# A strided-attention and gated-FFN kernel: h of the last seven chunks by seven block products of 256 columns (Strassen's identity)

## The chip, the cores and the metric

One core of one Trainium2 chip. The metric is device time in microseconds of one execution of the whole kernel; lower is better. The engines named below are TensorE (PE, with its weight loads PEld), VectorE (DVE), ScalarE (ACT), GpSimd (POOL) and SyncE (SP), which issues most transfers.

## The reference

Attention over 8 batches of 8 heads, 576 rows, width 64, with a local mask for heads 0 to 3 and a strided mask for heads 4 to 7; its output, seen as 4608 rows of 512, goes through a feed-forward layer with 2048 hidden columns.

```
scores = scale * np.matmul(q, k.transpose(0, 1, 3, 2))
mask_local = (rel >= 0) & (rel < 32)
mask_strided = (rel >= 0) & (pos[None, :] % 32 == pos[:, None] % 32)
attn = softmax(np.where(masks, scores, -1e9));  x = (attn @ v) as (4608, 512)
h = x @ w_in                                   # 512 -> 2048
sp = np.maximum(h, 0.0) + np.log1p(np.exp(-np.abs(h)))
g = h * erf(sp)
return g @ w_out                               # 2048 -> 512
```

## The kernel before, in words

x is worked on in nine chunks of 512 rows: chunk b (0 to 7) is the first 512 rows of batch b, and chunk 8 collects the 64 rows that each batch has left over, which `stash` puts into the DRAM tensor `rests` and `reload` brings back. A chunk has 16 f-tiles of 128 hidden columns. Every fp32 operand is held as two float32r parts, a high one and the low rest (`xhi`/`xlo`, `pair[:, 0]`/`pair[:, 1]`, `ghi`/`glo`), and a product is made of three matmul terms: high by high, low weight by high, high weight by low.

`ftile` (one per chunk and f-tile) issues, in this order of dependence: 12 matmuls of 512 columns for h (four blocks of 128 of x's 512 columns, three terms, L914) into a PSUM bank; a DVE copy `hs` out of that bank (L922); softplus and erf on ACT (L925, L928), each with a table load per two f-tiles; the product a*hs on DVE (L931); the split of the result into `ghi` on ACT (L934) and `glo` on DVE (L937); and 12 matmuls of 512 columns for the output (four banks o0 to o3 of 128 rows, three terms, L980). After the 16th f-tile ACT evacuates the four banks and SP stores them.

Attention for batches 2 to 7 runs between the f-tiles: `burst` is one run of TensorE that multiplies the weights of one pair of heads with v and makes the scores of the next pair; `Pair.soft` is the softmax between, over DVE, ACT and POOL, with a transpose and an exchange `pt<-tt` of quarters through SP (L766). The first two batches are done ahead of the f-tiles by `heads`. `weight` turns the 64-bit weights into the two float32r parts, on DVE (three bit operations and a subtraction on 128x1024) and ACT.

The order on each engine is written by `Plan.order()`, a list scheduler that starts, of the operations that are ready, the one with the lowest key; the keys are tables of numbers (`FE`, `FT`, `KP`, ...). Each engine then runs its list strictly in that order. While the first f-tiles wait, the plan fills TensorE with dummy matmuls `warm` (L1143).

Of the kernel before, what the change touches and what calls it, by code (L numbers as in the profile page):

```python
# [60 lines left out]
KP = (
    (-19.871, -19.772, -18.081, 66.367, -18.136, 66.385, -21.044),
    (-20, -19.783, -18.109, -17.925, 66.357, -18.175, 65.821),
    (-20.011, -20.022, -18.1, -17.903, -17.836, -17.915, -18.021),
    (-19.805, -19.783, -18.131, 65.874, 66.629, 66.053, 66.246),
    (-17.104, -8.328, 50.311, 2195.03794, 66.246, 102.21, 68.625),
    (-19.761, -19.772, 66.052, -18.121, -18.137, 102.19, 102.261),
    (-17.222, -16.968, 68.835, 66.436, 68.835, 50.29, -17.926),
    (-19.75, -19.88, 66.257, 68.556, 68.856, 66.235, 65.932),
    (-16.968, 102.961, 74.711, 2202.59494, 2202.66194, 2240.33894, 2239.52794),  # L70
    (66.961, 2240.52794, 160.089, 2239.27294, 2251.46194, 31.017, 102.239),
    (31.228, 2312.70894, 184.489, 146.19, 2428.50594, 103.15, 102.328),
    (2312.71994, 103.339, 208.889, 2293.98794, 2306.33394, 103.217, 207.07),
    (103.439, 2330.76494, 8023.49621, 2257.52794, 2312.35094, 237.161, 176.808),
    (2459.68094, 103.439, 245.489, 255.672, 236.95, 2434.38194, 2348.29394),
    (2330.75394, 103.428, 245.478, 2355.10594, 102.854, 2349.06194, 333.672),
    (237.518, 237.507, 294.289, 2294.26294, 2397.84494, 2397.86194, 2415.89494),
    (237.496, 103.45, 7811.28821, 2416.10594, 2434.37094, 341.673, 2300.35194),
    (334.761, 335.139, 343.089, 2446.64494, 2452.53794, 2397.66194, 2458.56994),
    (2301.36294, 2459.58094, 361.389, 2458.71894, 2428.48394, 102.843, 2409.99594),  # L80
    (2459.65894, 2459.58094, 391.889, 2410.20694, 2489.36694, 2397.75094, 2458.54794),
    (2459.65894, 2459.65894, 8103.71921, 2513.71694, 2647.99494, 2513.76194, 2531.83094),
    (2459.65894, 2593.93694, 440.689, 2532.02094, 2532.10994, 432.372, 2550.19594),
    (432.539, 432.528, 465.089, 377.967, 2556.41194, 341.973, 2568.36194),
    (433.262, 432.561, 483.389, 2568.57294, 2574.76694, 529.8, 529.45),
    (432.939, 432.561, 513.889, 2593.14494, 2599.13394, 2550.31194, 529.45),
    (573.961, 2593.92594, 538.289, 2623.41994, 529.95, 2629.68394, 572.839),
    (2661.09094, 573.95, 562.689, 2641.76194, 529.889, 2647.98394, 603.373),
    (530.439, 573.839, 574.889, 2568.76294, 529.939, 2647.97294, 603.483),
    (470.441, 2661.05794, 8229.05321, 603.532, 2648.06194, 725.161, 529.006),  # L90
    (573.828, 627.561, 635.889, 2733.27794, 2733.36694, 627.939, 724.25),
    (627.55, 2599.05394, 660.289, 2757.79494, 529.928, 2598.84294, 626.85),
    (823.161, 2599.03194, 678.589, 670.65, 670.7, 627.739, 724.35),
)
# [1162 lines left out]
```

## Time and profile before

| | |
|---|---|
| time, median of 3 runs | 891.66 us (891.28 to 893.11) |
| span of the profiled execution | 890.8 us |
| TensorE busy in it | 872.9 us, 7436 matmuls |
| VectorE, ScalarE busy | 504.0 us, 590.8 us |
| bytes moved by DMA | 75.24 MB |

The span runs from the first to the last instruction of the profiled execution; the median of the runs lies 0.9 us above it. A busy TensorE in the profile overlaps successive matmuls, so the rate of a stream is read from the starts of its matmuls in the timeline, not from the mean duration of one.

### The profile page before, as it was taken

To read this page: it belongs to the slowest core of one execution; us is meant where nothing else is said; L and a number is where in the kernel's file an instruction comes from. 1 tells how busy PE (TensorE), PEld (TensorE's weight loads), DVE (VectorE), ACT (ScalarE), POOL (GpSimd) and SP (SyncE) were. 2 spreads that over 40 slices of the span, in tenths; PEclk is the share of its full clock that TensorE was granted. 3 is DMA by queue.
4 is the path that set the end of the run, shared out by engine and by line. 5 is a ranking of instruction groups with operands and counts; after the bars stand their busy time and mean duration, and the time that the engine had idled before them with its cause. 6 is when DMAs were issued, how large, how long until landed. Compare 5 with 4: busy or idle time off the path is not lost.

```text
span 890.8 us, 18132 instructions
## 1 busy us (share of the span) xinstructions
PE 872.9 (98%) x7436; PEld 716.2 (80%) x7436; DVE 504.0 (57%) x799; ACT 590.8 (66%) x878; POOL 120.6 (14%) x157
## 2 busy tenths in 40 slices
PE   6899999999999999999999999999999999999997
PEld 4677888888888888888888888888888888888886
DVE  5989994556565555655555555555556433343432
ACT  4887786676676667666666677666766565466653
POOL 2210000132221110102112111121112200000000
PEclk9999999999999999999999999999999999999999
DMA  9997010151332122212321222112311310001001
GB/s 346 368 363 261 1 48 7 59 119 58 89 88 71 59 72 96 73 57 72 104 73 56 74 88 79 45 30 72 100 68 32 105 47 1 1 1 47 1 1 47
DMA packets 37266, 75.24 MB, mean 84 GB/s; under 512 B 12960, under 2 KB 16288, under 8 KB 37184
## 3 DMA queue, kind: packets, MB, share of 16 engines
q1 hardware_dynamic: 34576, 69.24, 23.0%
q0 software_dynamic: 2448, 4.59, 2.7%
q8 instruction: 58, 0.95, 0.4%
q10 hardware_dynamic: 160, 0.26, 0.1%
q14 instruction: 24, 0.20, 0.1%
HBM read 56.12 MB, written 13.63 MB: 78 GB/s over the span
## 4 chain that ended last, share of the span: by engine, by line
PE 69%; issue 21%; DVE 3%; ACT 3%; DMA 3%; SPq 0%; POOL 0%; POOLq 0%; ACTq 0%; DVEq 0%
PE h L914 32%; PE o L980 30%; PE x L682 3%; PE s L662 2%; DMA qk<-qk_str 1%; PE s L536 1%; DVE pair L883 1%; ACT L928 1%; ACT L925 1%; PE s L409 1%; DMA out<-ob 1%; PE s L516 0%; DVE a L931 0%; DVE w L869 0%; DMA rests<-xhi 0%
## 5 line engine op out<-in xcount | busy, mean ns | idle before, releaser
L980 PE MATMUL o<-pair,ghi 128*128 128x512 f32 x1152 | 358.2, 392 | 0.3 <-DVE xlo L560 0.3
L914 PE MATMUL h<-xhi,pair 128*128 128x512 f32 x1152 | 287.6, 392 | 1.3 <-DVE a L931 0.8
L914 PEld LDWEIGHTS h<-xhi,pair 128*128 128x128 f32 x1152 | 216.1, 188 | 48.4 <-DVE a L931 1.8
L980 PEld LDWEIGHTS o<-pair,ghi 128*128 128x128 f32 x1152 | 214.1, 188 | 45.7 <-DVE xlo L560 0.5
L980 PE MATMUL o<-pair,glo 128*128 128x512 f32 x576 | 224.3, 389 | 0.0
L934 ACT CAST ghi<-a 128x512 fp32r<-128x512 f32 x144 | 89.2, 621 | 169.8 <-PE o L980 155.0
L922 DVE COPY hs<-h 128x512 f32<-128x512 f32 x128 | 88.0, 687 | 131.6 <-PE h L914 131.5
L914 PE MATMUL h<-xlo,pair 128*128 128x512 f32 x576 | 155.0, 391 | 0.0
L937 DVE TENSOR_TENSOR glo<-a,ghi 128x512 fp32r<-128x512 f32 x144 | 100.7, 700 | 77.8 <-ACT ghi L934 75.7
L931 DVE TENSOR_TENSOR a<-a,hs 128x512 f32<-128x512 f32 x128 | 88.7, 730 | 88.6 <-ACT a L928 88.6
L914 PEld LDWEIGHTS h<-xlo,pair 128*128 128x128 f32 x576 | 108.7, 189 | 22.7
L980 PEld LDWEIGHTS o<-pair,glo 128*128 128x128 f32 x576 | 108.1, 188 | 22.6
L925 ACT ACT_TABLE_LOAD x83 | 106.5, 1283 | 21.9 <-DVE hs L922 20.7
L925 ACT ACTIVATE a<-hs 128x512 f32<-128x512 f32 x128 | 80.8, 632 | 54.5 <-DVE hs L922 46.9
L739 POOL TENSOR_TENSOR sm<-sm,r 128x640 f32<-128x640 f32 (+1 forms) x24 | 35.4, 1475 | 468.3 <-DVE r L736 433.3
L928 ACT ACT_TABLE_LOAD x72 | 92.4, 1283 | 1.3
L928 ACT ACTIVATE a<-a 128x512 f32<-128x512 f32 x144 | 83.8, 625 | 0.8
L761 POOL COPY pt<-tt 32x320 f32<-32x320 f32 (+1 forms) x96 | 57.8, 602 | 46.1 <-DVE tt L745 42.6
L719 DVE TENSOR_TENSOR s<-s,con 128x640 f32<-128x640 f32 (+1 forms) x24 | 21.6, 899 | 37.4 <-PE s L662 37.4
L745 DVE STREAM_TRANSPOSE tt<-sm 128x320 f32<-128x320 f32 (+1 forms) x48 | 23.2, 522 | 19.4 <-POOL sm L739 19.4
L682 PEld LDWEIGHTS x<-pt,v 64*64 64x64 f32 x1392 | 24.4, 134 | 8.5 <-issue 8.5
L728 ACT ACT_TABLE_LOAD x24 | 30.8, 1283 | 0.4
(68 smaller groups left out, 503.1 us busy)
## 6 DMA issues: line engine op xcount, KB each, us to landing
v<-v_loc SPq DMA_DIRECT2D x16, 640.0 KB, 5.4
qk<-qk_loc SPq DMA_DIRECT2D x16, 592.0 KB, 5.2
words<-w_in SPq DMA_DIRECT2D x8, 1024.0 KB, 11.3
words<-w_out SPq DMA_DIRECT2D x8, 1024.0 KB, 7.8
out<-ob SPq DMA_DIRECT2D x32, 256.0 KB, 2.3
qk<-qk_res SPq DMA_DIRECT2D x12, 656.0 KB, 5.7
v<-v_str SPq DMA_DIRECT2D x16, 384.0 KB, 4.4
qk<-qk_str SPq DMA_DIRECT2D x4, 608.0 KB, 7.9
```

The source lines that it names most:

```text
L682: yield nc.tensor.matmul(self.x[m][d, n * a : n * (a + 1)], self.v[rows, (2 * a + h) * D : (2 * a + h) * D + D], p, start=True, stop=True,)
L728: yield nc.scalar.activation(sm[:, :, :cols], sm[:, :, :cols], AF.Exp, scale=1.0 / D**0.5)
L739: yield nc.gpsimd.tensor_tensor(out=wide(sm), in0=wide(sm), in1=spread(rc), op=ALU.mult)
L761: yield nc.gpsimd.tensor_copy(pt[quarter(m, f), f, :], plane(m, f, f))
L914: yield nc.tensor.matmul(ph[:, :CH], win[f // 2][:, w, 2 * P * cc + f0 : 2 * P * cc + f0 + P], x[cc][:, c0 : c0 + CH], start=(lo and i == ...
L922: yield nc.vector.tensor_copy(hs.tile, ph.tile)
L925: yield nc.scalar.activation(a.tile, hs.tile, AF.Softplus)
L928: yield nc.scalar.activation(a.tile, a.tile, AF.Erf)
L931: yield nc.vector.tensor_tensor(out=a.tile, in0=a.tile, in1=hs.tile, op=ALU.mult)
L934: yield nc.scalar.copy(ghi.tile, a.tile)
L937: yield nc.vector.tensor_tensor(out=glo.tile, in0=a.tile, in1=ghi.tile.bitcast(F32), op=ALU.subtract)
L980: yield nc.tensor.matmul(po.tile, g[:, ts], wout[f // 2][:, w, f % 2 * SW : f % 2 * SW + SW], start=(f == first_f and i == 0), stop=(f == ...
```

## The change

Chunks 0 and 1 are done as before. From chunk 2 on, two f-tiles are done together by `fpair`. With the 512 rows of x in two halves of 256, the 512 inputs in two halves of 256 (each two blocks of 128) and the 256 hidden columns in two f-tiles, the 2x2 block product is made with Strassen's identity in Winograd's form: seven block products, each of 6 matmuls of 256 columns (three terms by two blocks of 128 inputs). So h of two f-tiles takes 42 matmuls of 256 columns (L1016) where it took 24 of 512. The second matmul (now `second`, L1168) stays as it is.

What this needs around it: `prepare` (once per pair of f-tiles and half) makes the four weight sums S1 to S4 on DVE and ACT and stores them with the three unchanged blocks into the DRAM tensor `blocks`; `stream` loads the seven blocks of a pair, 256 KB each, for every pair of every chunk, into two alternating sets of buffers; `convert` makes the sums of x's blocks and their high and low parts, once per chunk and half of the inputs, from an fp32 copy `raw` that ACT takes out of PSUM (L841) in place of the split; and `fpair` makes h out of the products in the two PSUM banks X and Y: one ACT copy (L1046), five DVE additions (L1037) and a DVE copy (L1056) of 128x256 take the place of the two `hs` copies. The keys of the plan are new throughout, those of the first chunks too.

```diff
+    def prepare(i, k, pair, ready, before, key):
+        ...
+        def sums():
+            a11, a12, a21, a22 = "S2", "S4", "S3", "S1"
+            for out, a, b, op in (("S1", a21, a22, ALU.add), ("S3", a11, a21, ALU.subtract),
+                                  ("S2", "S1", a11, ALU.subtract), ("S4", a12, "S2", ALU.subtract)):
+                yield nc.vector.tensor_tensor(out=piece(out), in0=piece(a), in1=piece(b), op=op)
...
+        o = add("dve", 0.15 + 4 * P / 960.0, key, whole, [ready, *before], [made], [pair])
+        o = add("dve", 4 * (0.1 + P / 960.0), key + 0.1, sums, [o], [], [made])
+        o = add("act", 0.2 + 4 * P / 1200.0, key - 2095.0, s_hi, [o], [], [made])
+        o = add("dve", 0.15 + 4 * P / 960.0, key + 0.2, s_lo, [o], [], [made])
+        out = [add("sp", P * 8 * SW / 3.9e5, key - 2090.0, store_made, [o], [], [made])]
...
+    def convert(c, k, raw, ready_a, ready_b, key):
...
+        o1 = add("dve", d, key, minus("t1", "b12", "b11"), ready_a, [], [raw])
+        o3 = add("dve", d, key + 0.01, minus("b12", "b22", "b12"), [o1, *ready_b], [], [raw])
+        o2 = add("dve", d, key + 0.02, minus("t2", "b22", "t1"), [o1, *ready_b], [], [raw])
+        o4 = add("dve", d, key + 0.03, minus("t4", "b21", "t2"), [o2], [], [raw])
+        out = []
+        for i, n, t, o in ((0, 4, ta, o3), (1, 3, tb, o4)):
+            o = add("act", 0.2 + n * HALF / 1200.0, key + CV[1] + 0.1 * i, hi(i), [o], [t], [raw])
+            out.append(add("dve", 0.15 + n * HALF / 960.0, key + 0.1 + 0.1 * i, lo(i), [o], [], [raw, t]))
...
+    def stream(n, j, key):
...
+        def load(dst, u, m=1):
+            def run():
+                yield nc.sync.dma_start(dst(), blocks_d[j][:, u : u + m])
...
+    def fpair(c, j, ts, ready, w_ready, after_burst):
...
+        def products(todo):
+            def run():
+                for dst, half, x, t, first in todo:
+                    w = unit(units, x)
+                    i, y = place[t]
+                    terms = [(p, q, kk) for p, q in ((0, 0), (1, 0), (0, 1)) for kk in range(2)]
+                    for e, (p, q, kk) in enumerate(terms):
+                        yield nc.tensor.matmul(
+                            dst[:, half * HALF : half * HALF + HALF], w[:, kk, p], ts[kk][i][:, y, q],
+                            start=first and e == 0, stop=e == len(terms) - 1, skip_group_check=True,
+                        )
...
+        p16 = pe(0, [(X, 0, "A11", "B11", True), (X, 1, "S2", "T2", False)], [*ready, *mm1_first[-1:], *after_burst], [X], [])
+        p57 = pe(1, [(Y, 0, "S1", "T1", True), (Y, 1, "S3", "T3", False)], [p16], [Y], [])
...
+        p1 = add("act", 0.2 + HALF / 1200.0, v0 + SUM[0], first_sum, [p16], [u], [X])
+        u2 = add("dve", d, v0 + SUM[1], plus(lambda: u[:, :HALF], lambda: X[:, HALF:], lambda: u[:, HALF:]), [p1], [], [X, u])
+        t5 = add("dve", d, v0 + SUM[1], plus(lambda: u[:, HALF:], lambda: Y[:, :HALF], lambda: u[:, :HALF]), [p57, u2], [], [Y, u])
+        c22 = add("dve", d, v0 + SUM[2], plus(lambda: u[:, HALF:], lambda: Y[:, HALF:], lambda: u[:, HALF:]), [t5], [], [Y, u])
+        p2 = pe(2, [(X, 0, "A12", "B21", False)], [p57, u2], [], [X])
+        p34 = pe(3, [(Y, 0, "S4", "B22", False), (Y, 1, "A22", "T4", False)], [p2, c22], [], [Y])
...
+        c11 = add("dve", d, v0 + SUM[3], keep, [p2, u2], [hs[0]], [X])
+        c12 = add("dve", d, v0 + SUM[3], plus(lambda: hs[0][:, HALF:], lambda: Y[:, :HALF], lambda: u[:, :HALF]), [p34, c11], [], [Y, u, hs[0]])
+        c21 = add("dve", d, v0 + SUM[4], plus(lambda: u[:, :HALF], lambda: Y[:, HALF:], lambda: u[:, :HALF]), [p34, c12], [], [Y, u])
```

The softplus, erf, product and split of the two f-tiles follow `c12` and `c21` as before. A burst of attention now stands after every second pair, and the products of the next pair stand behind it.

The order on TensorE in chunk 5 before: the last of h of one f-tile (h, L914), then the output matmuls (o, L980) of an earlier f-tile, then h of the next.

```order
L914 MATMUL h_5916<-xlo_83,pair_1123 128x512
L914 MATMUL h_5916<-xlo_84,pair_1123 128x512
L980 MATMUL o_80_5690<-pair_1345,ghi_5885 128x512 x2
L980 MATMUL o_80_5690<-pair_1345,glo_5887 128x512
L980 MATMUL o_80_5720<-pair_1345,ghi_5885 128x512 x2
L980 MATMUL o_80_5720<-pair_1345,glo_5887 128x512
L914 MATMUL h_5946<-xhi_77,pair_1455 128x512
```

The order on TensorE in chunk 5 now, at the third step of one pair: the end of the second step (hy is bank Y, L1016), the third step (hx is bank X), two groups of output matmuls (L1168), and the first two matmuls of the fourth step. ta_0 and ta_1 are the converted halves of x, u the streamed weight blocks.

```order
L1016 MATMUL hy_7438<-ta_0_5856,u_7182 128x256
L1016 MATMUL hy_7438<-ta_1_6557,u_7182 128x256
L1016 MATMUL hx_7418<-ta_0_5856,u_29_7306 128x256
L1016 MATMUL hx_7418<-ta_1_6557,u_29_7306 128x256
...
L1168 MATMUL o_80_6933<-pair_1417,ghi_7327 128x512 x2
L1168 MATMUL o_80_6933<-pair_1417,glo_7331 128x512
L1168 MATMUL o_80_6950<-pair_1417,ghi_7327 128x512 x2
L1168 MATMUL o_80_6950<-pair_1417,glo_7331 128x512
L1016 MATMUL hy_7438<-ta_0_5856,u_7182 128x256
L1016 MATMUL hy_7438<-ta_1_6557,u_7182 128x256
```

The h work of two f-tiles, which stood in two groups of 12 with output matmuls between, now stands in steps of 12, 12, 6 and 12 shorter ones, and the third step follows the second with nothing between; it has to wait for a sum on DVE that reads the first step's bank.

The order on DVE around the second and third prepared weight before: the products a (L931) and low parts glo (L937) of f-tiles 2 and 3 of the first chunk, among the weight work (L862 to L883).

```order
L875 SCALAR_TENSOR_TENSOR w_2_806<-words_531,w_2_806 128x1024
L931 TENSOR_TENSOR a_956<-a_956,h_808 128x512
L560 TENSOR_TENSOR xlo_81<-s_0_840,xhi_77 128x256
L560 TENSOR_TENSOR xlo_81<-s_0_840,xhi_77 128x320
L931 TENSOR_TENSOR a_947<-a_947,h_887 128x512
L883 TENSOR_TENSOR pair_1051<-w_9_942,pair_1051 128x1024
L937 TENSOR_TENSOR glo_1080<-a_947,ghi_1076 128x512
```

The same place on DVE now (L1254 is the product, L1260 the low part, L1120 to L1141 the weight work).

```order
L1141 TENSOR_TENSOR pair_940<-w_9_899,pair_940 128x1024
L1120 TENSOR_SCALAR w_3_1016<-words_915 128x1024
L1127 SCALAR_TENSOR_TENSOR w_3_1016<-words_915,w_3_1016 128x1024
L1133 SCALAR_TENSOR_TENSOR w_3_1016<-words_915,w_3_1016 128x1024
L1141 TENSOR_TENSOR pair_997<-w_2_925,pair_997 128x1024
L1120 TENSOR_SCALAR w_6_1075<-words_938 128x1024
L1141 TENSOR_TENSOR pair_1072<-w_3_1016,pair_1072 128x1024
L1127 SCALAR_TENSOR_TENSOR w_6_1075<-words_938,w_6_1075 128x1024
L1254 TENSOR_TENSOR a_1021<-a_1021,h_820 128x512
```

The eight weight operations shown, which stood behind the first of these products, now stand ahead of it. On TensorE 13 more `warm` matmuls stand in the stretch that follows (25 in all, 12 before), in runs of 5, 6 and 2 between the first chunks' f-tiles.

## Rows read from the trace of the kernel before

**Rows 1.** The page: span, busy time by engine, bytes per slice of a 40th.

```profile
span 890.8 us, 18132 instructions
PE 872.9 (98%) x7436; PEld 716.2 (80%) x7436; DVE 504.0 (57%) x799; ACT 590.8 (66%) x878; POOL 120.6 (14%) x157
PE   6899999999999999999999999999999999999997
GB/s 346 368 363 261 1 48 7 59 119 58 89 88 71 59 72 96 73 57 72 104 73 56 74 88 79 45 30 72 100 68 32 105 47 1 1 1 47 1 1 47
```

**Rows 2.** Busy time by engine in four stretches, granted clock, DMA.

```profile
core 0: us, PE busy (x) PEld busy (x) DVE busy (x) ACT busy (x) POOL busy (x), PEclk, DMA share, GB/s
0.00:50.00 50.00, 38.72 (x878) 29.21 (x878) 39.99 (x82) 32.42 (x125) 10.83 (x15) 0.90 0.97 362
50.00:150.00 100.00, 98.87 (x696) 80.55 (x695) 85.65 (x108) 76.86 (x114) 7.58 (x8) 1.00 0.36 130
350.00:450.00 100.00, 99.83 (x890) 82.07 (x890) 57.15 (x95) 67.60 (x90) 16.59 (x21) 1.00 0.22 68
750.00:891.00 141.00, 135.75 (x599) 112.06 (x598) 50.11 (x77) 79.39 (x105) 1.62 (x3) 1.00 0.05 16
```

**Rows 3.** Waits of TensorE, longest first: total us, times, longest.

```profile
PE s L409 <- DMA qk<-qk_str: 5.3, 2, 4.8
PE h L914 <- DVE a L931: 0.8, 1, 0.8
```

**Rows 4.** Groups by line and shape, TensorE and its weight loads: busy, mean ns.

```profile
L914 PE MATMUL h<-xhi,pair 128*128 128x512 f32 x1152 | 287.6, 392 | 1.3 <-DVE a L931 0.8 <-DVE hs L922 0.3
L980 PE MATMUL o<-pair,ghi 128*128 128x512 f32 x1152 | 358.2, 392 | 0.3 <-DVE xlo L560 0.3
L914 PEld LDWEIGHTS h<-xhi,pair 128*128 128x128 f32 x1152 | 216.1, 188 | 48.4 <-DVE a L931 1.8 <-DVE hs L922 1.7
```

**Rows 5.** Timeline, TensorE at 802 us: start, us, operation, idle before.

```profile
801.95 1.98 PE L914 MATMUL h<-xhi,pair 128*128 128x512 f32 x8
804.67 0.62 PE L980 MATMUL o<-pair,ghi 128*128 128x512 f32 x2
```

**Rows 6.** Timeline around one burst of attention at 412 us.

```profile
412.71 0.91 PE L682 MATMUL x<-pt,v 64*64 64x54 f32 x44
414.51 0.30 PEld L980 LDWEIGHTS o<-pair,ghi 128*128 128x128 f32 x2
414.51 0.73 PE L980 MATMUL o<-pair,ghi 128*128 128x512 f32 x2
```

**Rows 7.** Timeline, dummy matmuls in bf16 at 21.7 us.

```profile
21.74 0.81 PE L1143 MATMUL warm<-con 128*128 128x512 bf16 x3
```

**Rows 8.** Groups by line and shape, DVE.

```profile
L937 DVE TENSOR_TENSOR glo<-a,ghi 128x512 fp32r<-128x512 f32 x144 | 100.7, 700 | 77.8 <-ACT ghi L934 75.7 <-PE o L980 1.7
L922 DVE COPY hs<-h 128x512 f32<-128x512 f32 x128 | 88.0, 687 | 131.6 <-PE h L914 131.5
L883 DVE TENSOR_TENSOR pair<-w,pair 128x1024 fp32r<-128x1024 f32 x16 | 20.5, 1284 | 0.0
L869 DVE SCALAR_TENSOR_TENSOR w<-words,w 128x1024 uint32<-128x1024 uint32 x16 | 20.5, 1280 | 0.2
L862 DVE TENSOR_SCALAR w<-words 128x1024 uint32<-128x1024 uint32 x16 | 11.4, 713 | 2.0 <-DMA out<-ob 1.6 <-DMA words<-w_in 0.3
L830 DVE TENSOR_TENSOR xlo<-x,xhi 128x256 fp32r<-128x256 f32 x12 | 5.0, 415 | 0.0
```

**Rows 9.** Groups by line and shape, ACT.

```profile
L880 ACT CAST pair<-w 128x1024 fp32r<-128x1024 f32 x16 | 16.9, 1057 | 5.7 <-DVE w L875 5.3 <-issue 0.4
L825 ACT CAST xhi<-x 128x256 fp32r<-128x256 f32 x12 | 4.3, 359 | 0.0
```

**Rows 10.** Timeline, a hand-off from TensorE to DVE at 420 us.

```profile
419.18 1.07 PE L914 MATMUL h<-xlo,pair 128*128 128x512 f32 x4
420.28 0.69 DVE L922 COPY hs<-h 128x512 f32<-128x512 f32 x1 [0.63 <-PE h L914]
```

**Rows 11.** Timeline, the exchange of the softmax ahead of that burst.

```profile
403.36 2.41 SPq L766 DMA_DIRECT2D pt<-tt  x4
```

**Rows 12.** Transfers by issuing line: times, KB each, median us from issue to landing.

```profile
out<-ob SPq DMA_DIRECT2D x32, 256.0 KB, 2.3
```

More of the change, by code (lines that the diff above doesn't have):

```diff
@@ L69 @@
[L69 to L75, printed above, removed]
@@ L1067, in attention_moe @@
         wout.append(pair)
+    chain = w2[:]
+    prepared = [[o for k in range(2) for o in prepare(i, k, win[i], w1[i], chain, 2091.0 + PRO + SLOT * (P0 + PREP * i + PREP / 2 * k))] for i in range(NP)]
     def chunk(c, f0, f1):
@@ new lines, in attention_moe, with keys_of, step @@
+    last_av = []
+    put, halves, raws, copies = [], {}, {}, {}
+    place = lambda b, i: PRO + SLOT * 2 * (NP * (b - 1) + 2 * i + BURST) + AT[6]
+    pair = None
+    def keys_of(n):
+        b, i = divmod(n, 4)
+        if b < 3:
+            return KP[n]
+        v = place(b, i)
+        return (v + AT[0], v + AT[0] + 1.0, v, v + AT[1], v + AT[2], v + AT[3], v)
+    def step(n, before):
+        p, b, i = the[n], n // 4, n % 4
+        k = p.hp % 2
+        if p.hp < 2:
+            raws[b, k] = new_raw(b, k)
+        follow = the[n + 1] if n + 1 < 4 * B else None
+        if follow:
+            follow.loads()
+        p.key_c = p.keys[6] + 0.1 if b < 3 else place(b, i) + AT[5]
+        copies[b, p.hp] = burst(p, follow, before, raws[b, k])
+        if follow:
+            follow.soft()
+        c0 = p.hp // 2 * S + CH
+        raw = raws[b, k]
+        put.append(stash(b, p.hp, lambda: raw[:, c0 : c0 + REST], [raw], copies[b, p.hp], p.keys[2] + 1.0))
+        if p.hp >= 2:
+            key = PRO + SLOT * 2 * NP * b if k else p.key_c + 2 * SLOT
+            halves[b, k] = convert(b, k, raw, copies[b, k], copies[b, k + 2], key + 2080.0 if b < 3 else key + CV[0] if k else key)
+        return turns["b"], copies[b, p.hp]
@@ L1103, in attention_moe @@
+    the = {n: Pair(n // 4, ORDER[n % 4], keys_of(n)) for n in range(8, 4 * B)}
+    for n, p in the.items():
+        p.key_b = KB[n - 8] if n < 8 + len(KB) else p.keys[2]
+        p.key_e = KE[n - 8] if n < 12 else p.keys[2] + AT[4]
+    for b in range(B):
+        if b < 2:
+            for hp in range(4):
+                keys = KP[4 * b + hp]
+                banks, home, act_sum, pool_norm, fetch_by = PAIRS[4 * b + hp]
                 done, o_s, o, loads = heads(
@@ L1128, in attention_moe @@
                 chunk(c, f0, f1)
-        elif b > 1:
-            chunk(b, 0, NFC)
-        if b == B - 1:
-            free = [mm1_of[B - 2], *(o for n in put for o in put[n])]
-            x_of[B] = [reload(hp, n, x, free) for hp in range(NCC) for n, x in enumerate((xhi, xlo))]
-            chunk(B, 0, NFC)
+        elif b == 2:
+            the[8].loads()
+            burst(None, the[8], before=last_av)
+            the[8].soft()
+            for n in range(8, 12):
+                step(n, [])
+        if b >= 2:
+            wait = []
+            for j in range(NP):
+                ts = [halves[b, k] for k in range(2)]
+                o = fpair(b, j, ts, [x for h in ts for x in h[2]], [w2[j]], wait)
+                wait = []
+                if b + 1 < B and j % 2 == BURST:
+                    o, done = step(4 * (b + 1) + j // 2, [o] if FORCE else [])
+                    wait = [o] if FORCE else []
+    for k in range(2):
+        raw = new_raw(B, k)
+        v = PRO + SLOT * 2 * (NP * (B - 1) + 3 * k + 1)
+        os = [reload(k, raw, put, v)]
+        os.append(reload(k + 2, raw, os[:], v))
+        halves[B, k] = convert(B, k, raw, os[:1], os, v + CV[0])
+    for j in range(NP):
+        ts = [halves[B, k] for k in range(2)]
+        fpair(B, j, ts, [x for h in ts for x in h[2]], [w2[j]], [])
     def warm(tag):
```

496 lines of the change are left out of this document (324 added, 172 removed).

## The prediction

> **What bounds the kernel now.** I read the page first: TensorE is busy in 872.9 us of a span of 890.8, and in the row of slices only the first two and the last are not full [rows 1]. The windows show where the other 18 us lie: 11.3 in the first 50 us, 1.1 from 50 to 150, 5.3 in the last window, and 0.2 of 100 us in mid-kernel, always at the full clock after the start [rows 2]. The list of waits agrees: the longest is 5.3 us for the first loads, and of the steady part there is nothing over 0.8 [rows 3]. So in the seven chunks that change, time is TensorE's work and nothing else, and an edit is worth what it takes off that work, less the waits that it brings.
>
> The price of a matmul is read from starts, not from the mean of 392 ns, which overlaps its neighbour [rows 4]. In the timeline 12 matmuls of h begin at 801.95 and what follows begins at 804.67 [rows 5]: 2.72 us, 226.7 ns each. At 2.4 GHz 512 columns are 213.3 ns, so 13.3 ns come on top of the columns.
>
> **TensorE's saving.** Two f-tiles' h took 24 x 226.7 ns = 5.44 us; they now take 42 matmuls of 256 columns. No such matmul is in this trace, so its price is bounded. If the 13.3 ns go with the columns, it is half, 113.3 ns; if they come once per matmul, it is 106.7 + 13.3 = 120.0 ns. Per pair of f-tiles the saving is 5.44 - 4.76 = 0.68 us by the first and 5.44 - 5.04 = 0.40 us by the second, over 7 x 8 = 56 pairs 38.1 or 22.4 us. Three dummy matmuls in bf16 at 512 columns took 0.81 us with the last one's tail of 392 - 227 = 165 ns [rows 4, 7], 0.215 each, with weight loads between as here, so the 13.3 ns belong to fp32r but not plainly to either kind. I take the middle, 116.7 ns: 4.90 us a pair, 0.54 saved, 30.2 us in all.
>
> The weight load is the open point, because it no longer has 227 ns to hide in. One takes 188 ns [rows 4], longer than the matmul that is to cover it. But after a burst two loads of 188 ns together take 0.30 us [rows 6]: the second starts 0.11 us behind the first, when the first matmul starts. So a load is usable after about 110 ns and the rest is latency; it just fits under 113 to 120 ns.
>
> The Trainium skill (TensorE: Matmul & The Clock Gate, Part 3, The mechanism) says that a weight load overlaps matmuls in flight only when its row group differs, and these loads fill all rows. By that, with its 107 ns for 128 columns (LDWEIGHTS), a 512-column matmul would take 320 ns, and the change would go from 24 x 320 = 7.68 to 42 x 214 = 8.99 us a pair, 73 us lost by that estimate. The row of 226.7 ns refutes it at 512 columns; no row tests 256.
>
> **What is added on the other engines.** A pair of f-tiles, with half a burst (412.71 to 414.62, 1.9 us [rows 6]), takes 10.88 + 0.95 = 11.83 us now and 11.29 after. DVE is busy 57% [rows 2], 6.76 us a pair. Six sums of 256 columns come for two copies of 512: 6 x 0.415 - 2 x 0.687 = +1.12 us. Converting x is, per chunk, eight differences (3.3 us) and four low parts of 1024 and 768 columns (some 4.6, after the 1.284) for eight subtractions of mean 0.45 (3.6): +0.5 a pair [rows 8]. That makes 8.4 of 11.29, 74%. ACT at 67.6% is 8.0 us; one copy (0.36) and the casts of the conversion ((2 x 1.06 + 2 x 0.85) / 8 = 0.48 [rows 9]) make 8.84, 78%. Neither engine becomes the bound on its own; these 56 x 2.5 us cost nothing as long as TensorE has other work in front of it.
>
> DMA: seven loads of 256 KB a pair are 1.84 MB in 11.29 us, 163 GB/s, on top of 68; the queue has moved 362 in the first 50 us [rows 2]. At that rate the seven take 5.1 us, one 256 KB store lands in 2.3 [rows 12], and a buffer is free a whole pair ahead, over 10 us. I put this at nothing. The exchange of the softmax, on the same queue, had finished at 405.77 for a burst at 412.71 [rows 6, 11]: 6.9 us of cover, more than the seven loads ahead of it.
>
> **Where waits come.** In the order, the third step of a pair stands directly behind the second in 14 of 56 pairs, and it needs an ACT copy and a DVE sum on the first step's result. The hand-off: the last matmul outlives its turn by 0.165 us, and DVE starts 0.03 us later [rows 10]; then 0.36 + 0.415 and small hand-offs, about 1.05 us. The second step covers 12 x 116.7 = 1.40, a margin of 0.35. In 29 pairs the next pair's first step follows the fourth directly, and its second step needs two DVE sums that free bank Y: 0.165 + 0.03 + 0.83, against the same 1.40. So there are 43 tight places that hold if the engine is free and slip if it is in the middle of an operation of 0.7 us or more. Ends: 0 if the order has room everywhere; 43 x 0.7 = 30 us if each pays a whole operation [rows 8]. With the engines a quarter idle I take a third of the places at 0.35 us: 5 us.
>
> **The first chunks.** Their matmuls are the same, but the eight weight operations that now stand ahead of the third f-tile's product on DVE are 3 x 1.284 + 2 x 0.713 + 3 x 1.28 = 9.1 us [rows 8], in a stretch where DVE is 86% busy and TensorE has 1.1 us idle [rows 2]. The plan puts `warm` only where TensorE has nothing ready, and there are 13 more. A `warm` takes at least 0.215 us [rows 7], 2.8 us for 13; if all 9.1 us showed, that. I take 5. The 16 preparations on DVE (each about 2.3 us, 37 us) go into the following 100 us, where DVE had some 40% idle; their stores end before chunk 2 by the order. Nothing for them. In the last chunk's tail 19 groups of three output matmuls (12.9 us) stand between the last products and the first matmul that needs them, over a chain on ACT and DVE of some 7: nothing.
>
> **Sum.** 890.8 - 30.2 + 5 + 5 = 870.6 for the span, and 0.9 more for the runs: 871.5 us.
>
> **The rivals.**
> 1. *DVE and ACT come late at the tight places (the other side).* The two are busy 74 and 78% in strict order, and each of the 43 places is a chain through both. Against it: before, TensorE lost 0.2 us in 100. The saving left after the first chunks is 25.2 us, so it decides at 25.2 / 43 = 0.59 us a place; at a whole operation of 0.7 the time is 890.8 - 30.2 + 5 + 30 + 0.9 = 896.5.
> 2. *The weight load is not covered.* If a load had to end its 188 ns before the next matmul, 42 x 0.188 = 7.9 us a pair for 5.44: 56 x 2.46 = 138 us, some 1035 with the 5 of the first chunks. Even 130 ns a matmul ends the saving. For: 188 is above 120. Against: 110 ns after the burst [rows 6]. The rule on row groups above (the Trainium skill, TensorE: Matmul & The Clock Gate, Part 3, The mechanism) would push the same way.
> 3. *The streamed blocks come late.* SP runs its list in order, 532 entries for 193, and a load that waits for a buffer holds the exchange behind it. One us lost a pair is 56 us: 871.5 + 56 = 927. For: TensorE now waits for DMA in each pair. Against: 10 us ahead, at two thirds of the rate seen.
> 4. *Better than forecast:* without the 13.3 ns (109 ns with some issue), 4.58 us a pair, 48 us saved, 890.8 - 48 + 5 + 5 + 0.9 = 854.
>
> **Chances.** What a measurement of this kernel can tell from no change is about 0.2%, 1.8 us: faster means below 889.9, slower above 893.4. The forecast (113 to 120 ns, 3 to 9 us in the first chunks, 0 to 12 us of waits; 857 to 889 at the ends) has 0.67. Rival 1 has 0.15: half of it, with waits short of its deciding point, still faster, 0.04 the same, 0.04 slower. Rival 2 has 0.06, rival 3 0.06, both slower, rival 4 0.06. Faster 0.67 + 0.07 + 0.06 = 0.80, same 0.04, slower 0.16. The range takes the forecast's ends and the nearer part of rival 1 and leaves out rivals 2 to 4: 856 to 892.
>
> **What would show it.** In the profile after, 12 matmuls of 256 columns in 1.36 to 1.44 us from start to start; above 1.56 the saving is gone. Mid-kernel windows with TensorE waiting 1% or less, and its waits named as sums on DVE (rival 1 if they exceed 10 us), not as the streamed blocks (rival 3). Between 50 and 100 us some 3 to 9 us more TensorE idle or in `warm`. DVE at about 74% and ACT at 78% in mid-kernel, DMA at about 230 GB/s. The prediction is wrong if the matmul's price lies outside 113 to 120 ns, or if the waits at the tight places are longer than a part of an operation.

## The result and the profile after

The changed kernel takes 902.8 us (median of 4 runs, 899.97 to 904.34) against 892.0 (891.28 to 893.11): the ratio is 1.0122, with a 95% interval from 1.0101 to 1.0143. It is 1.2% slower; the forecast was 871.5, and the time lies outside its range.

The page of the changed kernel, the lines that answer to [rows 1]: span, busy time, slices.

```profile
span 900.4 us, 21008 instructions
PE 862.9 (96%) x8451; PEld 749.4 (83%) x8457; DVE 630.1 (70%) x1155; ACT 628.6 (70%) x968; POOL 121.1 (13%) x157
...
PE   5887989999999999999999999999999999999997
```

TensorE is busy 10 us less than before, and the span is 9.6 us longer: it waits more, and the slices say where, in the first seven of 40. The windows of the changed kernel (columns as in [rows 2]) give the sizes.

```profile
0.00:50.00 50.00, 35.51 (x867) 27.14 (x872) 36.24 (x76) 29.72 (x113) 12.75 (x17) 0.93 0.94 343
50.00:100.00 50.00, 41.83 (x428) 32.47 (x428) 45.50 (x60) 35.10 (x68) 9.24 (x9) 0.90 0.71 242
100.00:150.00 50.00, 46.28 (x201) 37.08 (x202) 47.02 (x70) 36.96 (x50) 4.83 (x5) 1.00 0.37 111
...
250.00:750.00 500.00, 498.74 (x5219) 446.29 (x5218) 346.14 (x661) 360.71 (x511) 75.69 (x104) 1.00 0.70 225
```

Mid-kernel TensorE is busy 498.7 of 500 us, DVE 69%, ACT 72%, DMA at 225 GB/s: the steady part is as the prediction drew it. From 50 to 150 us TensorE is busy 88.1 us where it was 98.9 [rows 2], and the granted clock falls between 50 and 100: 0.90 is a mean over the two levels of 1.2 and 2.4 GHz, and it was 1.00 in the kernel before. It was 0.50, the lower level, between 62.86 and 65.58 us, behind 1.4 us in which TensorE stood: six output matmuls of 512 columns took 2.72 us there, twice the 1.36 that six take at the full clock [rows 5]. The timeline places the two parts: the starts of f-tile 12 (the 13th to be issued) and of chunk 2, first in the kernel before, then in the changed one.

```profile
110.15 1.19 PE L914 MATMUL h<-xhi,pair 128*128 128x512 f32 x4
...
226.32 0.84 PE L914 MATMUL h<-xhi,pair 128*128 128x512 f32 x3
```

```profile
128.88 2.12 PE L1237 MATMUL h<-xh,pair 128*128 128x512 f32 x8 [2.64 <-DVE a L1254]
...
253.84 0.98 PE L1016 MATMUL hx<-ta,u 128*128 128x256 f32 x6 [0.61 <-DVE hs L1245]
```

f-tile 12 is 18.7 us late, chunk 2 27.5. From the start of chunk 2 to the end of the span it took 890.8 - 226.3 = 664.5 us, now 900.4 - 253.8 = 646.6. So the seven changed chunks gain 17.9 us, and the two that were not to change lose 27.5; the difference is the 9.6 of the span.

What the seven chunks gain is read from starts again. Timeline of the changed kernel, TensorE at 500 us:

```profile
500.42 0.88 PE L1016 MATMUL hx<-ta,u 128*128 128x256 f32 x6
...
503.29 0.88 PE L1016 MATMUL hx<-ta,u 128*128 128x256 f32 x6
504.01 0.63 PE L1168 MATMUL o<-pair,ghi 128*128 128x512 f32 x2
...
505.40 0.88 PE L1016 MATMUL hy<-ta,u 128*128 128x256 f32 x6
```

Thirty matmuls of 256 columns begin at 500.42 and what follows begins at 504.01: 3.59 us, 119.7 ns each. It is the upper bound of the prediction, the 13.3 ns once per matmul. Between 504.01 and 505.40 stand six matmuls of 512 columns: 1.39 us, 231.7 ns each instead of the 226.7 of [rows 5]. Behind narrower matmuls this group lost some 30 ns.

TensorE's waits from chunk 2 to the last microseconds, as [rows 3]:

```profile
PE hx L1016 <- DVE hs L1245: 0.6, 1, 0.6
PE hy L1016 <- DMA u<-blocks: 0.3, 1, 0.3
PE hx L1016 <- DMA u<-blocks: 0.2, 1, 0.2
```

Neither the tight places (rival 1), nor the weight load (rival 2), nor the streamed blocks (rival 3) cost anything here worth counting.

### The profile page after: what moved, and what is told of

Its sections match the earlier page's. It is cut to its first block, busy times and chain, and to the rows that moved or that the text cites. A ratio compares the mean times of both kernels' runs of the same rounds, so it can differ in the third digit from the quotient of the medians.

```text
span 900.4 us, 21008 instructions
## 1 busy us (share of the span) xinstructions
PE 862.9 (96%) x8451; PEld 749.4 (83%) x8457; DVE 630.1 (70%) x1155; ACT 628.6 (70%) x968; POOL 121.1 (13%) x157
## 4 chain that ended last, share of the span: by engine, by line
PE 56%; issue 26%; DVE 10%; DMA 5%; ACT 2%; SPq 1%; POOL 1%; POOLq 0%; DVEq 0%; ACTq 0%
PE o L1168 25%; PE hy L1016 12%; PE hx L1016 9%; PE h L1237 5%; DMA u<-blocks 3%; PE x L696 2%; PE s L676 2%; DMA qk<-qk_str 1%; DVE w L1127 1%; DVE w L1133 1%; DVE glo L1260 1%; DVE made L921 1%; DVE pair L1141 1%; DVE a L1254 1%; PE s L551 1%
## 5 line engine op out<-in xcount | busy, mean ns | idle before, releaser
L1168 PE MATMUL o<-pair,ghi 128*128 128x512 f32 x1152 | 362.5, 396 | 2.3 <-DVE xl L574 1.4
L1168 PEld LDWEIGHTS o<-pair,ghi 128*128 128x128 f32 x1152 | 206.7, 190 | 39.2 <-DVE xl L574 1.5
L1168 PE MATMUL o<-pair,glo 128*128 128x512 f32 x576 | 224.8, 390 | 0.0
L1168 PEld LDWEIGHTS o<-pair,glo 128*128 128x128 f32 x576 | 108.5, 188 | 24.2 <-DVE glo L1260 0.2
L1016 PE MATMUL hx<-ta,u 128*128 128x256 f32 x672 | 98.9, 283 | 0.9 <-DVE hs L1245 0.6
L1016 PE MATMUL hy<-tb,u 128*128 128x256 f32 x672 | 99.0, 283 | 0.3 <-DMA u<-blocks 0.3
L1016 PEld LDWEIGHTS hx<-ta,u 128*128 128x128 f32 x672 | 92.2, 190 | 8.2 <-issue 1.5
L1016 PE MATMUL hy<-ta,u 128*128 128x256 f32 x672 | 98.5, 282 | 0.0
L1016 PEld LDWEIGHTS hy<-ta,u 128*128 128x128 f32 x672 | 91.7, 191 | 4.1
L1037 DVE TENSOR_TENSOR u<-hy,u 128x256 f32<-128x256 f32 x168 | 71.2, 424 | 32.3 <-PE hy L1016 27.6
L1016 PEld LDWEIGHTS hy<-tb,u 128*128 128x128 f32 x672 | 89.5, 191 | 2.0 <-DMA u<-blocks 0.7
L1046 ACT COPY u<-hx 128x256 f32<-128x256 f32 x56 | 20.9, 373 | 96.2 <-PE hx L1016 96.1
L1237 PE MATMUL h<-xh,pair 128*128 128x512 f32 x256 | 69.4, 414 | 8.2 <-DVE a L1254 4.4
L1076 DVE TENSOR_TENSOR a<-a,hs 128x512 f32<-128x512 f32 x56 | 38.5, 687 | 48.0 <-ACT a L1073 48.0
L1237 PEld LDWEIGHTS h<-xh,pair 128*128 128x128 f32 x256 | 49.1, 196 | 22.8 <-DVE a L1254 6.2
```

The lines of the kernel that those rows point to most:

```text
L1016: yield nc.tensor.matmul(dst[:, half * HALF : half * HALF + HALF], w[:, kk, p], ts[kk][i][:, y, q], start=first and e == 0, stop=e == len( ...
L1037: yield nc.vector.tensor_tensor(out=out(), in0=in0(), in1=in1(), op=ALU.add)
L1046: yield nc.scalar.copy(u[:, HALF:], X[:, :HALF])
L1076: yield nc.vector.tensor_tensor(out=a[f].tile, in0=a[f].tile, in1=hs[f].tile, op=ALU.mult)
L1168: yield nc.tensor.matmul(po.tile, g[:, ts], wout[f // 2][:, w, f % 2 * SW : f % 2 * SW + SW], start=(f == first_f and i == 0), stop=(f == ...
L1237: yield nc.tensor.matmul(ph[:, :CH], win[f // 2][:, w, 2 * P * cc + f0 : 2 * P * cc + f0 + P], xs[c][x][cc][:, :CH], start=(lo and i == 0) ...
```

## The experiments

Three theories for the 27.5 us. **A**: they have two causes, the new order of the first chunks (weight operations ahead of the f-tiles' own work on DVE) and the weight sums on DVE. **B**: the sums alone. **C**: neither, but the new scheme itself. A kernel with the sums and its partner without them run in the same order on every engine, so that only the sums differ.

**e1: the sums left out, the order kept.**

```diff
         def whole():
-            ...
-            yield nc.vector.tensor_tensor(out=d, in0=own(0), in1=own(1), op=ALU.add)
+            yield from ()
...
         def s_hi():
-            yield nc.scalar.copy(made[:, 0], made[:, 1].bitcast(F32))
+            yield nc.scalar.copy(made[:, 0].rearrange("p (f q) n -> p q f n", q=2), own(0))
```

(`sums` and `s_lo` likewise yield nothing, and the stores take the half that is left twice.)

> The changed kernel in its own order, with the DVE work of the weight sums left out (the sums and their low parts are not made, and copies of the weights are stored in their place, so the output is not the reference's). Theory A, the first two chunks are late in two parts: 18.7 us by f-tile 12, before the first sum runs at 134 us, because weight operations stand ahead of the f-tiles' own work on DVE, and some 9 us more from the sums: 902.8 - 9 = 894 us (890 to 897), with f-tile 12 still near 128.9 us. Theory B, the 44.9 us of sums on DVE are the whole loss: 902.8 - 27 = 876 us. Theory C, the loss is in the seven changed chunks (stream, waits): no change, 903 us.

The sums of the changed kernel, groups of DVE by line and shape up to 260 us:

```profile
L921 DVE TENSOR_TENSOR made<-made 128x128 f32<-128x128 f32 x64 | 21.7, 339 | 1.9
...
L915 DVE TENSOR_TENSOR made<-pair 128x512 f32<-128x512 f32 x16 | 12.3, 770 | 0.3 <-DMA blocks<-made 0.2
...
L927 DVE TENSOR_TENSOR made<-made 128x512 fp32r<-128x512 f32 x16 | 10.8, 681 | 2.3 <-ACT made L924 2.1
```

Together they are 44.8 us, 2.8 for each of the 16 preparations (2.3 in the prediction). Measured without them: 894.0 us, ratio to before 1.0025 (1.0007 to 1.0044). f-tile 12 starts at 126.4 us, chunk 2 at 245.55: 8.3 us earlier than in the changed kernel. Of these, 2.4 us were there at f-tile 12, before the first sum (134.0 us in the changed kernel), so 5.9 fall to the sums; the medians differ by 8.8. From chunk 2 to the end it is 649.2. So 45 us of sums on DVE cost TensorE 6 to 9 us, and 19 us of the loss are there without them. The time is theory A's 894; B as the only cause falls, and so does C, which left nothing to the sums.

**e5: the order alone, in the kernel before.** Each operation of the first 16 f-tiles gets a place, and `Plan.order()` keeps to it; arithmetic and chunks are those of before.

```diff
+        op.at = at[n] if n < len(at) else None
+        if op.at is not None:
+            op.key = op.at - 1000.0
...
+                    can = [(o, n, t) for o, n, t in can if o is head or o.at is None]
```

> The kernel before, its arithmetic unchanged, with the operations of the first 16 f-tiles, the heads and the weights in the order of the changed kernel. No weight sums, no seven products. Theory A, the order of the first chunks alone loses some 19 us, whatever comes after it: f-tile 12 starts near 128 instead of 110.2 us, TensorE never gets it back, 891 + 17 to 21 = 908 to 912 us. Theory B, the sums are the loss and the order is only fitted to them: 891 to 894 us. Theory E, the lateness is made up later because DVE has its weight work done earlier: 891 to 897.

Measured: 915.7 us, ratio 1.0273 (1.0251 to 1.0295). In the profile f-tile 12 starts at 123.8 us, 13.6 us late (near 128 had been expected), and chunk 2 at 246.0, 19.7 us late; from there it is the kernel before (911.2 - 246.0 = 665.2). The last 6 us came behind the 16 f-tiles with places, where the plan ordered anew: between 150 and 200 us TensorE is busy 45.89 us in e5 and 50.00 in the kernel before. So without one block product the order costs some 14 us by f-tile 12, the larger part of the 18.7. It is not the whole order of the changed kernel: the bursts of attention got no places.

Why, f-tile 4 says. It needs the PSUM bank that the product `a` of f-tile 2 reads, and that product is the one behind the eight weight operations of the prediction. Both in the kernel before:

```profile
62.34 0.69 DVE L931 TENSOR_TENSOR a<-a,h 128x512 f32<-128x512 f32 x1
...
64.14 1.98 PE L914 MATMUL h<-xhi,pair 128*128 128x512 f32 x8
```

in the changed kernel, and f-tile 4 in e5:

```profile
72.94 0.69 DVE L1254 TENSOR_TENSOR a<-a,h 128x512 f32<-128x512 f32 x1 [0.80 <-ACT a L1251]
...
74.46 1.40 PE L676 MATMUL s<-qk 64*32 64x64 f32 x80 [4.24 <-issue]
75.78 3.78 PE L1237 MATMUL h<-xh,pair 128*128 128x512 f32 x8
```

```profile
70.05 3.78 PE L981 MATMUL h<-xhi,pair 128*128 128x512 f32 x8 [3.84 <-DVE a L998]
```

The product is 10.6 us late and f-tile 4 is 11.6 us late, where f-tile 3 was 1.5. In e5 TensorE waits for just this product. In the changed kernel the product itself waits for ACT in its last 0.8 us, behind the weight operations. There a burst of attention (L676) also stands ahead of f-tile 4; it starts 4.24 us after the matmuls before it, and the profile shows nothing that it waited for. Since the product had ended at 73.63, at most 2.1 us of f-tile 4's lateness are that wait's. Up to f-tile 4 DVE has done 27 weight operations instead of 18, 9.4 us more. The four weight operations up to the start of f-tile 12, in the kernel before (110.15 us):

```profile
L869 DVE SCALAR_TENSOR_TENSOR w<-words,w 128x1024 uint32<-128x1024 uint32 x13 | 16.8, 1293 | 0.2
L875 DVE SCALAR_TENSOR_TENSOR w<-words,w 128x1024 uint32<-128x1024 uint32 x13 | 15.9, 1226 | 0.1
L883 DVE TENSOR_TENSOR pair<-w,pair 128x1024 fp32r<-128x1024 f32 x12 | 14.6, 1216 | 0.0
L862 DVE TENSOR_SCALAR w<-words 128x1024 uint32<-128x1024 uint32 x13 | 9.3, 718 | 1.3 <-DMA out<-ob 0.9 <-DMA words<-w_in 0.3
```

and in the changed kernel (128.88 us):

```profile
L1127 DVE SCALAR_TENSOR_TENSOR w<-words,w 128x1024 uint32<-128x1024 uint32 x16 | 20.4, 1279 | 0.2
L1133 DVE SCALAR_TENSOR_TENSOR w<-words,w 128x1024 uint32<-128x1024 uint32 x15 | 18.7, 1258 | 0.1
L1141 DVE TENSOR_TENSOR pair<-w,pair 128x1024 fp32r<-128x1024 f32 x15 | 18.5, 1240 | 0.1
L1120 DVE TENSOR_SCALAR w<-words 128x1024 uint32<-128x1024 uint32 x16 | 10.7, 676 | 1.2 <-DMA words<-w_out 1.1
```

51 operations, 56.6 us, against 62, 68.3: at the same f-tile DVE has done 11.7 us more of weights, which only later f-tiles use; e5 has done 62 too. That is the larger part of what is lost up to here, not all of it. Two more things can be read, the burst's wait and matmuls at the lower clock behind waits: the 12 of f-tile 4 took 4.62 us (75.78 to 80.40) instead of 2.72, and the six output matmuls named above 1.4 us more. No run separates these. Here is how that looks in windows of e5, to be held against those of before (48.87, 50.00 and 50.00 us of 50 on TensorE in these three):

```profile
50.00:100.00 50.00, 41.06 (x390) 31.95 (x373) 45.86 (x58) 34.31 (x67) 4.00 (x3) 0.93 0.65 234
100.00:150.00 50.00, 47.74 (x210) 39.17 (x209) 35.24 (x45) 35.32 (x46) 3.61 (x5) 1.00 0.07 25
150.00:200.00 50.00, 45.89 (x423) 36.58 (x422) 23.02 (x38) 28.34 (x39) 3.78 (x5) 1.00 0.13 39
```

DVE's lead does come back, as idle time after 125 us. What TensorE missed does not: from 250 to 750 us it is busy 499.36 of 500, and there is no place to make it up.

**e2 and e3: the first 16 f-tiles of the changed kernel back in the order of before, with the sums and without.** The edit is that of e5 with the places of the kernel before.

> The changed kernel, with the operations of the first 16 f-tiles, of the heads and of the weights in the order of the kernel before, the sums kept. Theory A: f-tile 12 starts near 112 us again, but DVE still has some 234 us of work ahead of chunk 2, so the sums come late and chunk 2 starts at 242 to 248 us: 892 to 897 us. Theory B: no change, 903. Theory D, the new order alone is the loss: 902.8 - 19 to 24, 879 to 884 us.

> Both edits together (the sums left out, so not the reference's output, and the order of before for the first 16 f-tiles). Theory A: the two parts add up, chunk 2 starts within 6 us of the kernel before (226.3), and what is left is the gain of the changed chunks, 18 us: 874 to 881 us. Theory C: 895 or more. Theory B: as the sums alone, 876.

Measured: 903.7 us (1.0134, 1.0102 to 1.0167) and 895.9 (1.0055, 1.0034 to 1.0077). The expectations of A fail for both; the times are those given to B (903) and to C (895 or more). The starts show why neither follows. f-tile 12 is back at 108.0 and 109.1 us, so the loss of the order is gone, but f-tile 16 starts at 138.0 and 138.9 instead of 130.7, chunk 2 at 248.4 and 240.3, and the rest takes 653.8 and 653.9 us where the changed kernel takes 646.6. What stands behind the fixed part was ordered anew by the plan, and that order is worse, with the sums and without them. The pair still gives the price of the sums a second time, 248.4 - 240.3 = 8.1 us at chunk 2. That the old order can be had together with the changed chunks and without this loss is not shown.

All starts of these kernels together, from the timelines (us):

| | f-tile 3 | f-tile 4 | f-tile 12 | chunk 2 | f-tile 3 to 12 | f-tile 12 to chunk 2 |
|---|---|---|---|---|---|---|
| before | 51.42 | 64.14 | 110.15 | 226.32 | 58.7 | 116.2 |
| changed | 52.96 | 75.78 | 128.88 | 253.84 | 75.9 | 125.0 |
| e1, changed without sums | 49.42 | 72.89 | 126.44 | 245.55 | 77.0 | 119.1 |
| e5, before in the new order | 50.51 | 70.05 | 123.78 | 246.04 | 73.3 | 122.3 |
| e2, changed in the old order | 48.67 | 62.01 | 108.00 | 248.39 | 59.3 | 140.4 |
| e3, e2 without sums | 50.35 | 63.15 | 109.14 | 240.26 | 58.8 | 131.1 |

Executions of one order (changed, e1) differ by 3.5 us at f-tile 3, so stretches are compared, not starts. From f-tile 3 to 12, ahead of the first sum, the new order costs 14.5 to 18.3 us in three kernels, and with the old order put back it costs 0.1 and 0.6. From f-tile 12 to chunk 2 the sums cost 5.9 us (changed and e1) and 9.3 (e2 and e3). So the 27.5 us are 1.5 up to f-tile 3, 17.2 of the order, and 8.8 behind it, of which 2.9 stay without the sums and are not explained.

**e7, e8, e11, e12: the seven products only from chunk 3 or 4 on**, the earlier chunks in the order of before, the sums spread over chunks where DVE was 57% busy [rows 2]; then the same two without the DVE work of the sums.

```diff
+C0 = 3
...
-        n = NP * (c - 2) + j
+        n = NP * (c - C0) + j + C0 % 2
...
+        o.earliest = EAR[2 * i + k]
```

> The seven products from chunk 3 on instead of chunk 2; chunks 0 to 2 keep the order of the kernel before up to f-tile 23, and the sums are spread from 150 to 300 us. Theory A, the loss is what is put ahead of the changed chunks (order and sums on a full DVE): the first product starts within 8 us of chunk 3 in the kernel before (320.4 us), six chunks gain 6 x (94.1 - 91.6) = 15 us: 891 - 15 + 8 = 884 us (879 to 889), faster than before. Theory C, the loss of 27 us belongs to the change from one scheme to the other, wherever it stands: 891 - 15 + 27 = 903 us.

> The same from chunk 4 on, the sums spread over chunks 2 and 3, the order of before up to f-tile 40. Theory A: five chunks gain 12.5 us, the first product within 8 us of chunk 4 in the kernel before (414.5 us): 891 - 12.5 + 5 = 884 us (879 to 888). Theory C: 905 us.

> The kernel with seven products from chunk 4 on, in its own order, with the DVE work of the sums left out (copies of the weights stored in their place, so not the reference's output). Theory A, in chunks 2 and 3 TensorE waits for copies of h that stand behind sums on DVE (5.8 us in all there): chunk 4 starts at 416 to 419 us instead of 423.7, 896.2 - 6 = 890 us (888 to 892). Theory C, the change from one scheme to the other costs this itself: 896.

> The same with seven products from chunk 3 on: there the sums' waits are 6.3 us and an output bank held up for 2.7, so theory A has chunk 3 start 7 to 9 us earlier, at 329 to 331 us: 906.2 - 8 = 898 us (896 to 901). Theory C: 906.

| | time, us | ratio to before | first product | chunk of before starts | from there to the end; before |
|---|---|---|---|---|---|
| e7 | 906.2 | 1.0167 (1.0140 to 1.0195) | 338.0 | 321.95 | 567.3; 568.9 |
| e12, e7 without sums | 900.6 | 1.0102 (1.0075 to 1.0130) | 326.8 | 321.95 | 568.2; 568.9 |
| e8 | 896.2 | 1.0062 (1.0042 to 1.0081) | 423.7 | 417.4 | 469.3; 473.4 |
| e11, e8 without sums | 892.0 | 1.0012 (0.9993 to 1.0031) | 420.6 | 417.4 | 471.1; 473.4 |

(The 414.5 us in the expectations was worked out from a mean chunk; the trace has 417.4.) Theory A's numbers for e7 and e8, 884 us, are missed by 22 and 12. Two things were wrong in them. First, the sums cost time even where DVE is not full (64 to 87% busy in e7, 76 to 77% in e8, sums included): the first product is 11.2 and 3.1 us later with them, and counted from f-tile 12, ahead of them, 7.6 and 4.8 us. In the waits of TensorE in e8 from chunk 2 to 430 us the longest entry (1.3 us in e11, without the sums) is

```profile
PE h L1274 <- DVE hs L1282: 5.8, 7, 1.5
```

and the timeline of DVE there shows how such a wait comes about:

```profile
256.43 0.99 DVE L951 TENSOR_TENSOR made<-pair 128x512 f32<-128x512 f32 x1
257.45 1.91 DVE L957 TENSOR_TENSOR made<-made 128x128 f32<-128x128 f32 x4
259.27 1.28 DVE L1291 TENSOR_TENSOR a<-a,hs 128x512 f32<-128x512 f32 x2
260.57 0.69 DVE L1297 TENSOR_TENSOR glo<-a,ghi 128x512 fp32r<-128x512 f32 x1
261.18 0.68 DVE L1282 COPY hs<-h 128x512 f32<-128x512 f32 x1
```

2.9 us of sums stand first, three operations of f-tiles are late behind them, and then the copy that empties the only bank of h. Second, the changed chunks hardly gain: 1.6 us over six and 4.1 over five, where 2.5 each had been expected. In e7 TensorE is busy 93.85 us of 100 from 350 to 450 and 96.39 from 450 to 550, and the hand-off from the second step to the third is seen to slip:

```profile
422.39 0.88 PE L1053 MATMUL hy<-ta,u 128*128 128x256 f32 x6
425.42 0.98 PE L1053 MATMUL hx<-ta,u 128*128 128x256 f32 x6 [2.15 <-DVE u L1074]
```

That is the tight place of the prediction (the third step directly behind the second), which the order of the changed kernel holds and this one does not; waits by this name are 4.3 us in e7, a part of what is missing. So the gain of 17.9 us belongs to the products together with that order. Theory C's 903 is near e7's time, but e7 and e8 do not show it, since most of their late start goes with the sums; 4.8 and 3.3 us of lateness stay that no run explains.

**e9, e10: the sums on GpSimd**, which is 13% busy, in the changed kernel and in e8.

```diff
-            yield nc.vector.tensor_tensor(out=d, in0=own(0), in1=own(1), op=ALU.add)
+            yield nc.gpsimd.tensor_tensor(out=d, in0=own(0), in1=own(1), op=ALU.add)
```

> The changed kernel in its own order, with the weight sums and their low parts made on GpSimd instead of DVE. GpSimd took 1.42 us for a 128x640 product, so some 1.1 + 4 x 0.35 + 1.1 = 3.6 us a preparation, 58 us in the 120 us in which it is a fifth busy. Theory A, the sums cost what they take of DVE's time: as without them, 894 us (892 to 897). Rival P, the two engines hinder each other or the softmax products of GpSimd come late behind the sums: 903 us or more.

> The kernel with seven products from chunk 4 on, its sums on GpSimd too. There TensorE waited in chunks 2 and 3 for copies of h on DVE that stood behind sums, 9 us by chunk 4. Theory A: most of these go, chunk 4 starts at 416 to 419 instead of 423.7, 896.2 - 6 = 890 us (887 to 893). Rival P: 896 or more.

Measured: 916.5 us (1.0277, 1.0257 to 1.0298) and 903.1 (1.0124, 1.0105 to 1.0143), each worse than with the sums on DVE. e9's groups of GpSimd, then the longest of ACT's waits from 120 to 280 us:

```profile
L921 POOL TENSOR_TENSOR made<-made 128x128 f32<-128x128 f32 x64 | 32.5, 508 | 4.7
...
L915 POOL TENSOR_TENSOR made<-pair 128x512 f32<-128x512 f32 x16 | 22.7, 1418 | 3.3 <-DMA blocks<-made 3.1
L927 POOL TENSOR_TENSOR made<-made 128x512 fp32r<-128x512 f32 x16 | 20.9, 1309 | 8.1 <-ACT made L924 8.1
```

```profile
ACT made L924 <- POOL made L921: 30.4, 11, 4.6
```

A preparation takes 4.8 us instead of 2.8, and the cast of the sums on ACT, which stands where DVE's sums would be done, waits 30.4 us (12.4 from 100 to 260 us with the sums on DVE), with all of ACT behind it.

**e4 and e6: the price of a narrow matmul by itself.** In the kernel before, h of chunks 2 to 8 in two matmuls of 256 columns, or four of 128, for each of 512.

```diff
+                n = CH // (PARTS if c >= 2 else 1)
                 for i, (w, x, cc) in enumerate(terms):
+                    for u in range(0, CH, n):
```

> The kernel before, with each 512-column matmul of h from chunk 2 on made as two of 256 columns with the same weights. If a matmul has 13.3 ns on top of its columns (120.0 ns at 256): 112 f-tiles x 12 x 13.3 ns = 17.9 us, and some 3 us for the change between the two widths: 892 + 18 to 22 = 910 to 914 us. If the price goes with the columns (113.3 ns): 892 to 895. If the weight load is what bounds a 256-column matmul here (130 ns or more): over 937.

> The kernel before, with each 512-column matmul of h from chunk 2 on made as four of 128 columns, each with its own weight load. If a matmul costs its columns and 13.3 ns, 66.7 ns each: 112 x 12 x (4 x 66.7 - 226.7) ns = 53.8 us more, 945 to 948 us. If a weight load has to follow the one before it by 110 ns or so, as the two loads behind a burst did [rows 6]: 112 x 12 x (440 - 226.7) ns = 287 us more, some 1178 us. Fully loaded in turn (188 ns): 1600 us.

Measured: 911.5 us (1.0219, 1.0190 to 1.0247) and 1189.6 (1.3349). Timelines, e4 and then e6:

```profile
603.64 2.08 PE L917 MATMUL h<-xhi,pair 128*128 128x256 f32 x16
605.55 1.12 PE L917 MATMUL h<-xlo,pair 128*128 128x256 f32 x8
606.51 0.63 PE L983 MATMUL o<-pair,ghi 128*128 128x512 f32 x2
```

```profile
602.84 3.68 PE L917 MATMUL h<-xhi,pair 128*128 128x128 f32 x32
606.36 1.95 PE L917 MATMUL h<-xlo,pair 128*128 128x128 f32 x16
608.15 0.68 PE L983 MATMUL o<-pair,ghi 128*128 128x512 f32 x2
```

24 matmuls in 2.87 us are 119.6 ns each; 48 in 5.31 are 110.6, where columns and 13.3 ns would be 66.7. At 128 columns the price is thus that of a weight load, the 0.11 us that [rows 6] showed, and at 256 columns the matmul's own, 9 ns above it.

## Why the prediction was wrong, step by step

**The failing step is "The first chunks", taken at 5 us; it is 27.5.** Both of its terms were mis-sized. The first is the weight operations moved ahead on DVE. Their count was right (eight, 9.1 us; by the trace DVE is 9 operations, 9.4 us, ahead at f-tile 4). Their price was not: 5 us lay between the 2.8 us of the 13 added dummies and the 9.1, as if the dummies told how long TensorE would have nothing ready. They tell what the plan expected. In the trace the whole length shows at once, 10.1 us from f-tile 3 to f-tile 4, and 17.2 us are lost by f-tile 12 (14.5 in e5, without any block product). The rows had no cover for it, with TensorE idle 1.1 us of 100 and DVE 86% busy. The sign named for it came true, 7.0 us more idle time between 50 and 100 us (48.87 - 41.83; 3 to 9 named), and was too weak: f-tile 8 is 15.9 us late, for idle time does not count matmuls at the lower clock, nor the 1.5 us up to f-tile 3. The second term, the sums, was set at nothing, since DVE had some 40% idle; they cost 6 to 9 us (e1; e3 against e2). The idle time was compared with the work in amount alone; TensorE needs DVE at given moments, and e8 shows sums in front of such a moment.

**TensorE's saving**, taken at 30.2 us, is 56 x (5.44 - 42 x 0.120) = 22.4: the upper bound of 120.0 ns holds (119.7 in the changed kernel, 119.6 in e4). Right in mechanism, 7.8 us off in size, because the middle was taken between two prices, of which one held.

**Waits in the steady part**, taken at 5 us: the gain of 17.9 lies 4.5 below 22.4. Listed waits are 1.1; the slow start of 512-column groups behind narrow ones, 0.03 us at two to three places in each of 56 pairs, would be 3 to 5, an estimate. e4 bears it out: of the 20.4 us that it is slower, the narrow matmuls are 112 x 12 x (2 x 119.6 - 226.7) ns = 16.8, and 3.6 are left, 0.03 for each of 112 changes of width (its interval is some 2.5 us either way). In e1, which has the same order, the gain is 15.3, so 17.9 is good to some 3 us. The size came out right by luck, since the cause was another: the tight places hold in this order and slip in e7.

**The rest was right:** DVE 69% (74 forecast), ACT 72% (78), DMA 225 GB/s (230), the stream at nothing, the weight load covered. In e6 a matmul of 128 columns, 53 ns at 2.4 GHz, comes each 110.6 ns while its load's record lasts 192 (188 in [rows 4]). The rule cited for rival 2 (the Trainium skill, TensorE: Matmul & The Clock Gate, Part 3, The mechanism: a weight load overlaps matmuls in flight only when its row group differs, taken without the background weight buffer that the section also names) does not hold for these full-height loads. The 110 ns came out, though the row was read a little beyond itself: the record of the first matmul begins at 414.51 us with the first load, not with the second at 414.62.

**The sum by the measured terms**: 890.8 - 22.4 + 4.5 + 27.5 = 900.4 us, the span measured; it closes by construction, as 4.5 and 27.5 are read from the same starts. The forecast's upper end was added up short: 890.8 - 22.4 + 9 + 12 + 0.9 is 890.3, not 889.

**Open:** the shares of the lead, the burst's wait and the lower clock in the 17.2 us; whether a better order could keep the sums and lose less than 17.9 us before chunk 2. None of the versions tried here beats the kernel before.

## What to carry to other kernels

Where the bound engine is full from some point on, a microsecond that it loses earlier is lost for good, so a change in the late stages is paid in the stage that prepares it: count, at several milestones, what the engine that it waits for has done by then, before and after, and take what stands ahead of an urgent operation there at its full length. Idle time of an engine covers added work only if no one waits for that engine in the meantime; ask which hand-off stands behind each added block. Halving the columns of a matmul halves its price only above the fixed part and the weight load, here 13.3 ns and 110 ns.
